# Second MoE of an attention and MoE chain: the first product as seven half-size products over halves of 256 tokens, Ln and Exp written into PSUM over h, output products one group later

## The chip, the cores and the metric

One Trainium2 chip, one of its cores. The time is device microseconds of one launch, inputs and outputs in HBM. Runs of the kernel before: median 1537.43 us of 3, from 1536.83 to 1538.73. One more execution was taken with the hardware profiler: 1537.71 us.

## The reference, cut to what matters

Attention first packs 576 keys into 32 per head and batch, and its output goes through two MoE blocks. The change is in the second:

```python
def _moe2_ref(x, w_in, w_out, a, b):          # x: 4608 x 512
    h = x @ w_in                              # 512 x 2048
    h2 = h * h
    h3 = h2 * h
    P = a[0] + a[1] * h + a[2] * h2 + a[3] * h3
    Q = 1.0 + np.abs(b[0]) * np.abs(h) + np.abs(b[1]) * h2
    g = P / (Q + 1e-06)
    return (g @ w_out).astype(np.float32)     # 2048 x 512
```

The first MoE has two products into 1536 features (gate and value) and one back to 512. All is f32. The kernel keeps a number as two f16 parts (high and low) and makes a product in three passes, high x high, high x low, low x high (`PASSES`).

## The kernel before, in words

The batches 0 to 7 go through attention and the first MoE. Its output x2 is written to HBM as two f16 parts, laid out in NB = 9 blocks of 512 tokens. All that up to the last batch is issued step by step in the order of one long string (`ORDER`): each word names a step of a few instructions. Every engine runs its own instructions in the order in which the program issues them, so this string sets the order of each engine and of the DMA queue. Beside the batches, the weights of the second MoE are decoded (they come as 64-bit words), split and stored to HBM: 16 tiles of w_in and 16 of w_out.

The last batch's gate and value tiles follow (L1127), with the loads of the 32 weight tiles, and then the second MoE, in plain loops. A chunk is 128 features of h for a block of 512 tokens; a block has 16. `h_mm` (L1414) makes a chunk in one PSUM bank: 12 matmuls of 512 columns. `stage_a` takes |h| and a linear term from it (ScalarE, L1426, L1427), then Q's first step on GpSimd (L1429), P's two steps on VectorE (L1432, L1433, which read h from PSUM) and Q's second step on VectorE (L1434). `stage_b`, one chunk later, has Ln and Exp (L1442, L1443, into SBUF) for 1/Q and three VectorE instructions (L1444 to L1446, all operands in SBUF). `stage_c`, two chunks later, splits g into two f16 parts (ScalarE L1451, GpSimd L1452).

The output product (`o_mm`, L1485) of a block runs one block behind: after chunk c of block j, TensorE makes chunk c of block j-1 for its four token tiles, 12 matmuls of 512 columns into four banks. At the block's end the four banks are evicted by ScalarE and VectorE (L1477, L1479) and stored. During block 0 the rest of the first MoE's output product (L1188) takes that place. The last block's output product comes at the end, one token tile after the other.

Of the kernel before, what the change touches and what calls it, by code (L numbers as in the profile page):

```python
# [1568 lines left out]
```

## Time and profile before

| | |
|---|---|
| profiled execution | 1537.71 us |
| its span, first to last instruction | 1535.9 us |
| TensorE busy | 1485.9 us (97%) |
| VectorE busy | 1304.3 us (85%) |
| ScalarE busy | 920.4 us (60%) |
| GpSimd busy | 576.7 us (38%) |
| granted TensorE clock, mean | 0.986 |

Busy times are shares of the whole span. The kernel has three stretches that differ: a start with many loads, the batches up to about 742 us, and the second MoE from there. A share says little about any one of them, so the rows below are taken by stretch. In the profile's rows PE is TensorE, DVE is VectorE, ACT is ScalarE and POOL is GpSimd. A clock of 1.00 is 2.4 GHz, 0.50 is 1.2 GHz.

### The profile page before, as it was taken

To read this page: it belongs to the slowest core of one execution; us is meant where nothing else is said; L and a number is where in the kernel's file an instruction comes from. 1 tells how busy PE (TensorE), PEld (TensorE's weight loads), DVE (VectorE), ACT (ScalarE), POOL (GpSimd) and SP (SyncE) were. 2 spreads that over 40 slices of the span, in tenths; PEclk is the share of its full clock that TensorE was granted. 3 is DMA by queue.
4 is the path that set the end of the run, shared out by engine and by line. 5 is a ranking of instruction groups with operands and counts; after the bars stand their busy time and mean duration, and the time that the engine had idled before them with its cause. 6 is when DMAs were issued, how large, how long until landed. Compare 5 with 4: busy or idle time off the path is not lost.

```text
span 1535.9 us, 28044 instructions
## 1 busy us (share of the span) xinstructions
PE 1485.9 (97%) x10644; PEld 887.6 (58%) x10644; DVE 1304.3 (85%) x2224; ACT 920.4 (60%) x1871; POOL 576.7 (38%) x663
## 2 busy tenths in 40 slices
...
GB/s 259 224 188 138 95 150 124 107 104 144 170 163 189 161 193 165 191 145 239 101 16 37 1 56 0 55 1 30 26 1 55 1 55 0 56 1 28 1 28 28
DMA packets 221911, 143.06 MB, mean 93 GB/s; under 512 B 162256, under 2 KB 199120, under 8 KB 220624
## 3 DMA queue, kind: packets, MB, share of 16 engines
...
## 4 chain that ended last, share of the span: by engine, by line
PE 80%; DVE 10%; DMA 3%; issue 2%; ACT 2%; POOL 1%; SPq 1%; POOLq 0%; DVEq 0%; ACTq 0%
PE h L1414 23%; PE o L1485 22%; PE o L1188 15%; PE gv L1127 13%; PE xo L891 1%; PE mm L417 1%; PE mm L415 1%; PE s L857 1%; DVE w L1444 1%; PE pk L811 1%; POOL y L1157 1%; DVE t L1145 1%; DVE v L749 1%; DVE t L1142 1%; DVE x16in L749 1%
## 5 line engine op out<-in xcount | busy, mean ns | idle before, releaser
L1485 PE MATMUL o<-w2o,g 128*128 128x512 f16 x1728 | 398.4, 381 | 6.5 <-DVE osb L1479 3.8
L1414 PE MATMUL h<-xi,w2i 128*128 128x512 f16 x1728 | 396.3, 379 | 0.0
L1127 PE MATMUL gv<-an,mt 128*128 128x256 f16 (+1 forms) x2304 | 305.2, 287 | 11.2 <-DVE t L1145 2.8
L1485 PEld LDWEIGHTS <-g 128*128 128x128 f16 x1728 | 169.4, 98 | 214.7 <-issue 8.8
L1188 PE MATMUL o<-y,wo 128*128 128x256 f16 (+1 forms) x2160 | 282.6, 286 | 2.8 <-POOL y L1157 1.9
L1414 PEld LDWEIGHTS <-w2i 128*128 128x128 f16 x1728 | 169.1, 98 | 200.9
L1127 PEld LDWEIGHTS <-mt 128*128 128x128 f16 x2304 | 222.0, 98 | 80.8 <-issue 25.7
L1188 PEld LDWEIGHTS <-wo 128*128 128x128 f16 x2304 | 224.5, 98 | 69.1 <-issue 7.2
L1157 POOL TENSOR_TENSOR y<-t,y 128x256 f16<-128x256 f32 (+1 forms) x180 | 151.9, 851 | 265.9 <-ACT y L1152 258.3
L1429 POOL TENSOR_SCALAR w<-ah,cf 128x512 f32<-128x512 f32 x144 | 110.6, 768 | 373.4 <-DVE t L1446 153.2
L1452 POOL TENSOR_TENSOR g<-t,g 128x512 f16<-128x512 f32 x144 | 174.5, 1211 | 99.5 <-issue 67.0
L1426 ACT ACTIVATE ah<-h 128x512 f32<-128x512 f32 x144 | 85.6, 594 | 207.4 <-PE h L1414 207.2
L1444 DVE SCALAR_TENSOR_TENSOR w<-w,r 128x512 f32<-128x512 f32 x144 | 180.0, 1250 | 3.9 <-ACT r L1443 3.9
L1434 DVE TENSOR_TENSOR w<-w,ah 128x512 f32<-128x512 f32 x144 | 134.9, 937 | 0.0
L1432 DVE TENSOR_TENSOR t<-t,h 128x512 f32<-128x512 f32 x144 | 98.4, 684 | 42.3 <-ACT t L1427 41.8
L1138 ACT ACTIVATE t<-gv 128x256 f32<-128x256 f32 (+1 forms) x192 | 76.6, 405 | 82.4 <-PE gv L1127 63.0
L1427 ACT ACTIVATE t<-h,cf 128x512 f32<-128x512 f32 x144 | 111.4, 774 | 22.5 <-POOL g L1452 22.3
L1142 DVE SCALAR_TENSOR_TENSOR t<-t,gv 128x256 f32<-128x256 f32 (+1 forms) x192 | 84.9, 448 | 40.1 <-ACT t L1138 39.3
L1433 DVE SCALAR_TENSOR_TENSOR t<-t,cf,h 128x512 f32<-128x512 f32 x144 | 107.7, 748 | 5.1
L1445 DVE SCALAR_TENSOR_TENSOR t<-t,cf,r 128x512 f32<-128x512 f32 x144 | 107.5, 747 | 0.0
L1446 DVE SCALAR_TENSOR_TENSOR t<-w,t 128x512 f32<-128x512 f32 x144 | 99.6, 692 | 4.9
L1442 ACT ACTIVATE r<-w,one 128x512 f32<-128x512 f32 x144 | 103.3, 717 | 0.0
...
## 6 DMA issues: line engine op xcount, KB each, us to landing
...
```

The lines of the kernel that those rows point to most:

```text
L1127: nc.tensor.matmul(out=ps, lhsT=mt[b, nm, c // 4, g][:, l, cs], rhs=an[b][:, 2 * r_ + g, cols], start=(n == 0), stop=(n == 5))
L1157: nc.gpsimd.tensor_tensor(out=y[:, 1], in0=t, in1=y[:, 0], op=ALU.subtract)
L1188: nc.tensor.matmul(out=ps, lhsT=wo1[c][:, l, d * 128:(d + 1) * 128], rhs=ys[b, h, c][:, r_, :], start=(c == 0 and n == 0), stop=(c == NF1 ...
L1414: nc.tensor.matmul(out=ps, lhsT=w[:, l, cs], rhs=x2in[j][:, r_, kc, :], start=(n == 0), stop=(n == 3 * KC - 1))
L1427: act(out=t, in_=ps, func=AF.Identity, scale=cf[:, 0:1], bias=cf[:, 7:8])
L1429: nc.gpsimd.tensor_scalar(out=w, in0=ah, scalar1=cf[:, 6:7], scalar2=cf[:, 5:6], op0=ALU.mult, op1=ALU.add)
L1433: stt(out=t, in0=t, scalar=cf[:, 1:2], in1=ps, op0=ALU.add, op1=ALU.mult)
L1434: nc.vector.tensor_tensor(out=w, in0=w, in1=ah, op=ALU.mult)
L1444: stt(out=w, in0=w, scalar=Q1, in1=r0, op0=ALU.add, op1=ALU.mult)
L1445: stt(out=t, in0=t, scalar=cf[:, 2:3], in1=r0, op0=ALU.add, op1=ALU.mult)
L1452: nc.gpsimd.tensor_tensor(out=g[:, 1], in0=t, in1=g[:, 0], op=ALU.subtract)
L1485: nc.tensor.matmul(out=ps, lhsT=gs[j, c][:, l, t * 128:(t + 1) * 128], rhs=w2t["o", 0, c][:, r_, :], start=(c == 0 and n == 0), stop=(c == ...
```

## The change

With x as halves of 256 tokens by halves of 256 inputs, and w_in as halves of 256 inputs by halves of 1024 features, the four quarters of h are sums of seven products instead of eight (Strassen's scheme in Winograd's form). A group (j, cp) is the unit now: two feature chunks in each half of the features, both token halves, so four banks A, B, C, D of 512 columns (two chunks of 256 tokens in each). A block has four groups; there are 36.

- Weights: seven combinations of w_in's quarters, 28 tiles instead of 16, made on GpSimd from the decoded tiles, split and stored as before; with w_out 44 tiles are stored and loaded.
- Tokens: x2 is kept as f32 in HBM (one ScalarE instruction evicts it, the VectorE instruction L1166 is gone). Per block four sums on VectorE (s3 to s6) and seven splits (h0 to h6 on ScalarE, l0 to l6 on GpSimd) make the seven operands.
- Products: 84 matmuls of 256 columns per group. Products 1, 6, 7 and 4 are added up in bank A, and ScalarE copies A to SBUF after 1, 6 and 7 (k1, k2, k3); 5 and 3 go into B, 2 into C. VectorE adds the copies: a1 writes bank D from B, a2 adds to C, a3 to B.
- Rational function: steps A (|h| and the linear term), w and W (Q on GpSimd, both steps), t and u (P), l and x (Ln and Exp, now into the bank of h), q, e, g (VectorE), h and i (the split). The number behind the letter is the tile, 0 to 3 for A, D, C, B.
- Output products: o0 to o3 in pieces of three matmuls, issued among the next group's products. f and F evict and store a token tile.
- Order: all of the kernel is issued from the string, which is new throughout. PSUM keeps 5 + 3 banks: three for A, B, C, five for D and the four output tiles.

```diff
-    x2_dram = [tc.dram_tile((128, 2, KC, BLK), F16, name=f"x2s{j}") for j in range(NB)]
+    x2_dram = [tc.dram_tile((128, KC, BLK), F32, name=f"x2s{j}") for j in range(NB)]
...
-        "wl2 wb2 wc2 wd2 0pl 0pf 0ph wl3 wb3 wc3 wl0 L0 0kf00 wb0 0kf01 0kg00 0kg01 wc0 L1 0kf02 wd3 0kf10 wd0 cc "
...
+        "wl9 wb9 0pl 0pf 0ph L1 0kf10 0kf12 0kg10 0kg12 wl7 wc9 wd9 0kf11 0kg11 0am1 cc L0 0kf00 wb7 0kg00 0kf01 "
...
+    def operands(j):
...
+        def hi(n, src):
+            act(out=flat(n, 0), in_=src(), func=AF.Copy)
...
+        def lo(n, src):
+            nc.gpsimd.tensor_tensor(out=flat(n, 1), in0=src(), in1=flat(n, 0), op=ALU.subtract)
+
+        def both(out, a, b, op):
+            nc.vector.tensor_tensor(out=out, in0=a, in1=b, op=op)
...
+        def product(x, p, e, first):
+            if first and e == 0:
+                bank(x)
+            fr, cs = divmod(2 * cp + e, 4)
+            n = 0
+            for kc in range(2):
+                w = w2t["t", p, 2 * fr + kc]
+                for l, r_ in PASSES:
+                    nc.tensor.matmul(
+                        out=st[x][:, W2 * e:W2 * e + W2], lhsT=w[:, l, 128 * cs:128 * cs + 128],
+                        rhs=xs[j][:, OPERAND[p], r_, kc], start=(first and e == 0 and n == 0), stop=(n == 5), skip_group_check=True,
+                    )
+                    n += 1
+
+        def keep(nm, x):
+            st[nm] = f32_tile("su")
+            act(out=st[nm], in_=st[x], func=AF.Copy)
+
+        def plus(out, a, b):
+            nc.vector.tensor_tensor(out=out, in0=a, in1=b, op=ALU.add)
+
+        for x, p, first in (("A", 1, True), ("A", 6, False), ("A", 7, False), ("A", 4, False), ("B", 5, True), ("C", 2, True), ("B", 3, False)):
...
-        nc.vector.tensor_tensor(out=w, in0=w, in1=ah, op=ALU.mult)
...
+        def s_q2():
+            nc.gpsimd.tensor_tensor(out=st["w", n], in0=st["w", n], in1=st["ah", n], op=ALU.mult)
...
-        r0 = st_p.tile([128, BLK], F32, tag="raw32", bufs=2, name="r0")
-        act(out=r0, in_=w, func=AF.Ln, bias=one[:, 0:1])
-        act(out=r0, in_=r0, func=AF.Exp, scale=-1.0)
-        stt(out=w, in0=w, scalar=Q1, in1=r0, op0=ALU.add, op1=ALU.mult)
-        stt(out=t, in0=t, scalar=cf[:, 2:3], in1=r0, op0=ALU.add, op1=ALU.mult)
-        stt(out=t, in0=w, scalar=-2.0, in1=t, op0=ALU.add, op1=ALU.mult)
...
+        def s_ln():
+            act(out=st[x], in_=st["w", n], func=AF.Ln, bias=one[:, 0:1])
+
+        def s_exp():
+            act(out=st[x], in_=st[x], func=AF.Exp, scale=-1.0)
+
+        def s_num():
+            stt(out=st["t", n], in0=st["t", n], scalar=cf[:, 2:3], in1=st[x], op0=ALU.add, op1=ALU.mult)
+
+        def s_err():
+            stt(out=st[x], in0=st["w", n], scalar=Q1, in1=st[x], op0=ALU.add, op1=ALU.mult)
+
+        def s_g():
+            stt(out=st["t", n], in0=st[x], scalar=-2.0, in1=st["t", n], op0=ALU.add, op1=ALU.mult)
```

In the middle of a later block the string repeats itself. The words of one group there (83: block 8, group 3; 82: the group before), product steps m, output pieces o:

```
g83m10 g82e1 g82A3 g82w2 g83m11 g82g1 g81o300 g82W2 g82t2 g83k1 g81o310 g82h1 g82u2 g83m60 g82i1 g82t3 g82l2 g83m61
...
g83m50 g83u0 g83W0 g83m51 g82o110 g82i3 g83l0 g83a1 g82o101 g83A1 g83m20 g83x0 g83m21 g83t1 g83w1 g82o111 g83q0 g83W1
```

ScalarE, the second MoE before: one chunk after the other, five instructions each (L1442 Ln, L1443 Exp, L1451 the high part, L1426 |h|, L1427 the linear term).

```order
L1442 ACTIVATE r_18130<-w,one 128x512 [waits DVE_49]
L1443 ACTIVATE r_18130<-r_18130 128x512 [waits Activation_49]
L1451 ACTIVATE g<-t_18036 128x512 [waits DVE_49]
L1426 ACTIVATE ah<-h 128x512 [waits PE_49]
L1427 ACTIVATE t_18165<-h,cf 128x512 [waits Pool_49]
```

ScalarE now, where one group ends and the next begins: Ln and Exp of tile 1 (hd is bank D), the linear pairs of tiles 2 and 3 (L1726, L1728), the first copy k1 of the next group's bank A (L1693), the high part of tile 1 and Ln of tile 2.

```order
L1745 ACTIVATE hd<-w,one 128x512 [waits DVE_49,Pool_49]
L1748 ACTIVATE hd<-hd 128x512 [waits Activation_49]
L1726 ACTIVATE ah<-h 128x512 [waits DVE_49]
L1728 ACTIVATE t<-h,cf 128x512
L1726 ACTIVATE ah<-h 128x512 [waits DVE_49]
L1728 ACTIVATE t<-h,cf 128x512
L1693 ACTIVATE su<-h 128x512 [waits PE_49]
L1761 ACTIVATE g<-t 128x512 [waits DVE_49]
L1745 ACTIVATE h<-w,one 128x512 [waits DVE_49,Pool_49]
```

The copy of bank A is a new kind of instruction for ScalarE, and it stands behind two linear pairs that wait for VectorE; on TensorE product 6 waits for it.

VectorE now, in the same stretch: a1 (L1696, into hd), step t of tile 1, q, e, g of tile 0, step u of tile 1, the two sums a2 and a3, and q, e, g of tile 1.

```order
L1696 TENSOR_TENSOR hd<-h,su 128x512
L1739 TENSOR_TENSOR t<-t,hd 128x512
L1751 SCALAR_TENSOR_TENSOR t<-t,cf,h 128x512
L1754 SCALAR_TENSOR_TENSOR h<-w,h 128x512
L1757 SCALAR_TENSOR_TENSOR t<-h,t 128x512
L1742 SCALAR_TENSOR_TENSOR t<-t,cf,hd 128x512
L1696 TENSOR_TENSOR h<-h,su 128x512 x2
L1751 SCALAR_TENSOR_TENSOR t<-t,cf,hd 128x512
L1754 SCALAR_TENSOR_TENSOR hd<-w,hd 128x512
L1757 SCALAR_TENSOR_TENSOR t<-hd,t 128x512
```

Every one of these has an operand in PSUM (h, hd); the sums are new, and the product of w and ah is no longer here.

GpSimd before, in the second MoE: two instructions by turns.

```order
L1429 TENSOR_SCALAR w<-ah,cf 128x512
L1452 TENSOR_TENSOR g<-t_18251,g 128x512
```

GpSimd now, in the first group of a block: three instructions per tile (L1731 and L1736 for Q, L1765 the low part of g), and between them low parts of the next block's operands (L1633, into xo).

```order
L1731 TENSOR_SCALAR w<-ah,cf 128x512
L1736 TENSOR_TENSOR w<-w,ah 128x512
L1633 TENSOR_TENSOR xo<-sx,xo 128x512
L1633 TENSOR_TENSOR xo<-xf,xo 128x512
L1765 TENSOR_TENSOR g<-t,g 128x512
L1633 TENSOR_TENSOR xo<-sx,xo 128x512
L1731 TENSOR_SCALAR w<-ah,cf 128x512
L1736 TENSOR_TENSOR w<-w,ah 128x512
L1765 TENSOR_TENSOR g<-t,g 128x512
L1633 TENSOR_TENSOR xo<-xf,xo 128x512 x2
```

The product L1736 came from VectorE, and the operand parts are gathered in one group of the four.

## Rows read from the trace of the kernel before

**Rows 1.** Table of stretches; stretch in us, its length, busy time of each engine (instructions).

```profile
core 0: us, PE busy (x) PEld busy (x) DVE busy (x) ACT busy (x) POOL busy (x), PEclk, DMA share, GB/s
0.00:100.00 100.00, 72.46 (x600) 46.74 (x600) 75.02 (x166) 48.26 (x114) 21.63 (x34) 0.85 0.77 228
100.00:704.00 604.00, 592.16 (x6014) 446.25 (x6015) 505.02 (x1116) 394.91 (x957) 252.33 (x314) 0.99 0.66 149
704.00:742.00 38.00, 38.00 (x314) 30.47 (x312) 23.40 (x54) 20.45 (x52) 19.44 (x27) 1.00 0.76 274
...
819.00:1481.00 662.00, 658.24 (x3047) 297.91 (x3045) 619.46 (x781) 397.82 (x651) 251.40 (x256) 1.00 0.07 23
1481.00:1536.00 55.00, 48.01 (x207) 20.30 (x205) 12.23 (x16) 7.68 (x13) 4.26 (x4) 0.94 0.12 39
```

**Rows 2.** Chain that ended last: start us, us, engine, tile, line, matmuls.

```profile
744.71 2.62 PE o L1188 x24
...
1085.08 2.59 PE o L1485 x12
...
1478.96 2.60 PE h L1414 x12
```

**Rows 3.** Order in time, one chunk: start us, us, engine, line, operation, out<-in, shapes.

```profile
1204.75 2.75 PE L1485 MATMUL o<-w2o,g 128*128 128x512 f16 x12
1204.95 0.60 ACT L1426 ACTIVATE ah<-h 128x512 f32<-128x512 f32 x1 [2.13 <-PE h L1414]
...
1205.44 0.77 ACT L1427 ACTIVATE t<-h,cf 128x512 f32<-128x512 f32 x1
1206.10 0.72 ACT L1442 ACTIVATE r<-w,one 128x512 f32<-128x512 f32 x1
1206.25 0.69 DVE L1432 TENSOR_TENSOR t<-t,h 128x512 f32<-128x512 f32 x1 [0.16 <-ACT t L1427]
1206.27 0.77 POOL L1429 TENSOR_SCALAR w<-ah,cf 128x512 f32<-128x512 f32 x1 [2.12 <-ACT t L1427]
1206.85 0.63 ACT L1443 ACTIVATE r<-r 128x512 f32<-128x512 f32 x1
1206.97 0.75 DVE L1433 SCALAR_TENSOR_TENSOR t<-t,cf,h 128x512 f32<-128x512 f32 x1
...
1207.39 0.61 ACT L1451 ACTIVATE g<-t 128x512 f16<-128x512 f32 x1
1207.63 0.68 DVE L1434 TENSOR_TENSOR w<-w,ah 128x512 f32<-128x512 f32 x1
1208.14 1.19 POOL L1452 TENSOR_TENSOR g<-t,g 128x512 f16<-128x512 f32 x1 [1.11 <-issue]
1208.23 1.65 DVE L1444 SCALAR_TENSOR_TENSOR w<-w,r 128x512 f32<-128x512 f32 x1
...
1209.81 0.74 DVE L1445 SCALAR_TENSOR_TENSOR t<-t,cf,r 128x512 f32<-128x512 f32 x1
...
1210.58 0.69 DVE L1446 SCALAR_TENSOR_TENSOR t<-w,t 128x512 f32<-128x512 f32 x1
```

**Rows 4.** One line's instructions: engine, count, duration ns min/median/max, first and last start.

```profile
L1432 DVE TENSOR_TENSOR t<-t,h x144: 677/682/690, 746.0 to 1482.9; 128x512 f32<-128x512 f32 x144
...
L1444 DVE SCALAR_TENSOR_TENSOR w<-w,r x144: 676/1645/1650, 753.2 to 1493.0; 128x512 f32<-128x512 f32 x144
```

**Rows 5.** The same view for L1166 and L375.

```profile
L1166 DVE SCALAR_TENSOR_TENSOR x2e<-o,x2e x64: 406/438/492, 127.5 to 818.8; 128x256 f16<-128x256 f32 x32, 128x320 f16<-128x320 f32 x32
...
L375 ACT ACTIVATE xo<-xo x35: 567/582/598, 166.5 to 702.6; 128x512 f32<-128x512 f32 x28, 64x512 f32<-64x512 f32 x7
```

**Rows 6.** Groups by line: count | busy us, mean ns | idle before, us.

```profile
L1321 POOL TENSOR_TENSOR raw<-raw,raw 128x512 f16<-128x512 f32 x32 | 40.4, 1264 | 50.2 <-ACT raw L1317 34.1 <-DVE x2e L1166 6.3 <-DVE sum L331 4.3
```

**Rows 7.** Order in time: the end of a block, and the last block's output product.

```profile
903.52 1.46 PE L1485 MATMUL o<-w2o,g 128*128 128x512 f16 x6 [0.54 <-DVE osb L1479]
...
1498.02 33.78 PE L1485 MATMUL o<-w2o,g 128*128 128x512 f16 x145 [0.25 <-POOL g L1452]
```

More of the change, by code (lines that the diff above doesn't have):

```diff
@@ L1327, in w2_pieces, with add, minus_of @@
         steps = {}
-        for n in range(len(w2_items)):
-            for nm, f in (
-                ("uL", lambda n: w2.load(n, nc.sync)), ("ub", w2.step), ("uc", w2.step), ("ud", w2.step),
-                ("uA", w2_scale), ("uH", w2_hi), ("uP", w2_lo), ("uS", w2_store),
+        def add(tag, key, src, dst):
+            for nm, f in zip("HPS", w2_split(key, src, dst)):
+                steps[f"u{nm}{tag}"] = f
+        def minus_of(out, a, b):
+            return lambda: nc.gpsimd.tensor_tensor(out=out(), in0=a(), in1=b(), op=ALU.subtract)
@@ L1384, in attention_pack_glu_rational_kernel @@
-    assert not w2_left and len(w2.dec) == len(w2_items)
-    last1 = itertools.chain(out1_slots(B - 1, 0), out1_slots(B - 1, 1))
-    an_p.release()
-    mt_p.release()
-    xi_p = sb("xi", "right")
-    g_p = sb("g", "left")
-    t2_p = sb("t2", "left")
-    ps_h = tc.alloc_tile_pool(name="ps_h", bufs=3, space=PSUM, side="right", reuse_waits="tile")
-    x2in = {}
-    def load_x2(j):
-        if j < NB:
-            t = xi_p.tile([128, 2, KC, BLK], F16, tag="xi", bufs=2, name="xi")
-            nc.sync.dma_start(out=t, in_=x2_dram[j])
-            x2in[j] = t
@@ L1403, in attention_pack_glu_rational_kernel @@
-    nc.scalar.preload_act_table_set("natural_log_exp_and_others")
-    gs = {}
-    pend = {}
-    def h_mm(j, c):
-        ps = ps_h.tile([128, BLK], F32, tag="h", name="h")
-        n = 0
-        for kc in range(KC):
-            w = w2t["i", c // 4, kc]
-            cs = slice((c % 4) * 128, (c % 4) * 128 + 128)
-            for l, r_ in PASSES:
-                nc.tensor.matmul(
-                    out=ps, lhsT=w[:, l, cs], rhs=x2in[j][:, r_, kc, :], start=(n == 0), stop=(n == 3 * KC - 1)
-                )
-                n += 1
-        return ps
@@ L1455, in late, with w2_load @@
-    def late(i):
-        if 0 <= i - 1 < NB * NF2:
-            stage_b(*divmod(i - 1, NF2))
-        if 0 <= i - 2 < NB * NF2:
-            stage_c(*divmod(i - 2, NF2))
-    one = const.tile([128, 1], F32, name="one")
-    nc.vector.memset(one, Q1)
+    NG = NF2 // 4
+    LAST = B - 1
+    one = const.tile([128, 1], F32, name="one")
+    Q1 = 1.0 + 1e-6
+    nc.vector.memset(one, Q1)
+    p2 = {}
+    late = []
+    xs, gs, po = {}, {}, {}
+    def w2_load(key):
+        t = w2t[key] = w2_p[0].tile([128, 2, 512], F16, name="w2{}_{}_{}".format(*key))
+        nc.sync.dma_start(out=t, in_=w2_dram[key])
@@ new lines, in attention_pack_glu_rational_kernel, with group, bank, mid @@
+    OPERAND = (None, 0, 1, 6, 2, 3, 4, 5)
+    TILES = ((1, 0), (1, 1), (0, 0), (0, 1))
+    def group(j, cp):
+        st = {}
+        steps = {}
+        W2 = BLK // 2
+        def bank(x):
+            if x == "D":
+                st[x] = ps_m.tile([128, BLK], F32, tag="m", name="hd")
+            else:
+                st[x] = ps_h[0].tile([128, BLK], F32, tag="h", bufs=3, name="h")
+        def product(x, p, e, first):
[9 more added lines that the diff above has]
+                        rhs=xs[j][:, OPERAND[p], r_, kc], start=(first and e == 0 and n == 0), stop=(n == 5), skip_group_check=True,
+                    )
+                    n += 1
[5 more added lines that the diff above has]
+        for x, p, first in (("A", 1, True), ("A", 6, False), ("A", 7, False), ("A", 4, False), ("B", 5, True), ("C", 2, True), ("B", 3, False)):
+            for e in range(2):
+                steps[f"m{p}{e}"] = lambda x=x, p=p, e=e, first=first: product(x, p, e, first)
+        steps["k1"] = lambda: keep("s1", "A")
+        steps["k2"] = lambda: keep("u2", "A")
+        steps["k3"] = lambda: keep("u3", "A")
+        def mid():
+            bank("D")
+            plus(st["D"], st["B"], st["u3"])
+        steps["a1"] = mid
+        steps["a2"] = lambda: plus(st["C"], st["C"], st["s1"])
+        steps["a3"] = lambda: plus(st["B"], st["B"], st["u2"])
+        for n, x in enumerate("ADCB"):
+            rational(steps, st, n, x, j, cp)
+        for n in range(4):
+            e, f = TILES[n]
+            for t in range(2):
+                for i in range(2):
+                    steps[f"o{n}{t}{i}"] = lambda n=n, t=2 * e + t, u=t, i=i, c=2 * cp + 8 * f + i: o_mm(j, t, gs[j, cp, n], u, i, c)
+        return {f"g{j}{cp}{nm}": f for nm, f in steps.items()}
@@ L1471, in token_rows @@
         return [(0, 128, rows[r])]
[L1473 to L1483 removed]
+    done = {}
@@ L1484, in o_mm @@
+    def o_mm(j, t, g, u, i, c):
+        k = j, t
+        if k not in po:
+            po[k] = ps_m.tile([128, DM], F32, tag="m", name="o")
+            done[k] = 0
         for n, (l, r_) in enumerate(PASSES):
             nc.tensor.matmul(
-                out=ps,
-                lhsT=gs[j, c][:, l, t * 128:(t + 1) * 128],
-                rhs=w2t["o", 0, c][:, r_, :],
-                start=(c == 0 and n == 0),
-                stop=(c == NF2 - 1 and n == 2),
-            )
-    ps_o = [None]
@@ L1524, in attention_pack_glu_rational_kernel @@
-    for i in range(2):
-        late(NB * NF2 + i)
-    for t in range(4):
-        ps = ps_o[0].tile([128, DM], F32, tag="o", name="o")
-        for c in range(NF2):
-            o_mm(ps, NB - 1, t, c)
-        finish(NB - 1, t, ps, "act" if t % 2 else "dve")
-    for pool in (t2_p, g_p, x2_p, tmp_p, y_p, wo1_p, st_p, const, xi_p, w2_p, yl_p[0], ps_o[0], ps_h):
+                out=po[k], lhsT=g[:, l, 256 * i + 128 * u:256 * i + 128 * u + 128], rhs=w2t["o", 0, c][:, r_, :],
+                start=(done[k] == 0), stop=(done[k] == 3 * NF2 - 1),
+            )
@@ new lines, in o_mm, with o_evict, o_store @@
+            done[k] += 1
+    osb = {}
+    def o_evict(j, t):
+        if t % 2:
+            o = st_p.tile([128, 512], I64, tag="raw64", bufs=STAGES, name="osb").bitcast(F32)[:, 0:DM]
+        else:
+            o = st_p.tile([128, DM], F32, tag="raw32", bufs=2, name="osb")
+        osb[j, t] = o
+        sc = 1.0 / (S_G * S_WO2)
+        if t % 2:
+            act(out=o, in_=po[j, t], func=AF.Copy, scale=sc)
+        else:
+            nc.vector.tensor_scalar_mul(o, po[j, t], sc)
+    def o_store(j, t):
+        for p0, n, dst in token_rows(4 * j + t):
+            nc.sync.dma_start(out=dst, in_=osb[j, t][p0:p0 + n])
@@ new lines, in attention_pack_glu_rational_kernel @@
+    for x in w2_keys:
+        p2["wL{}{:x}{:x}".format(*x)] = lambda x=x: w2_load(x)
+    for j in range(NB):
+        p2 |= operands(j)
+        for cp in range(NG):
+            p2 |= group(j, cp)
+        for t in range(4):
+            p2[f"f{j}{t}"] = lambda j=j, t=t: o_evict(j, t)
+            p2[f"F{j}{t}"] = lambda j=j, t=t: o_store(j, t)
+    steps |= p2
+    w2_p, xf_p, xo_p = [], [], [None, None]
+    seg = [x.split() for x in ORDER.split("|")]
+    for nm in seg[0]:
+        steps[nm]()
```

283 lines of the change are left out of this document (144 added, 139 removed), and 547 rows, old and new, of the table ORDER.

## The prediction

> **What bounds the kernel now.** I read the table of stretches first, then the chain of waits, then the order in time of one chunk, then the spread of single lines.
>
> In the table [rows 1] the reader is to see that TensorE is never free for long. In the second MoE (819 to 1481 us) it is busy 658.24 of 662.00 us at a granted clock of 1.00, the 2.4 GHz level. From 100 to 704 us it lacks 11.84 us. Only the first 100 us (27.5 us idle, clock 0.85) and the last 55 (7.0 us idle, clock 0.94) are worse. VectorE follows closely: 619.46 us of the same 662.
>
> The chain of waits [rows 2] says the same with prices. In the second MoE it runs through TensorE alone, tile after tile of 12 matmuls in 2.59 us, so a matmul of 512 columns costs 0.2158 us. The first MoE's matmuls of 256 columns, each with its own weight load, take 2.62 us for 24, so 0.1092 us. That is 1.2% over half, and it is what half-width products pay.
>
> The order in time of one chunk [rows 3] shows why TensorE could not simply be made faster before: a chunk's two tiles take TensorE 5.18 us, and VectorE's six instructions add up to 5.20. One of the six is swollen: L1444 takes 1.65 us, and began 0.09 us after GpSimd's L1452 (1.19 us). Its spread is 676 to 1650 ns, while L1432, which takes h from PSUM, stays within 677 to 690 ns though GpSimd's L1429 runs beside it [rows 3, 4].
>
> **The change, part by part.**
>
> *First product.* 1728 matmuls of 512 columns go: 1728 x 0.2158 = 372.9 us. 9 blocks x 4 groups x 84 = 3024 of 256 columns come: 3024 x 0.1092 = 330.2 us. **-42.7 us** of TensorE, which is on the path throughout. The 1728 of the output product stay. TensorE's floor for a group (four tiles) becomes 84 x 0.1092 + 48 x 0.2158 = 19.53 us, against 20.72 before. That only counts if three other engines stay under 19.53.
>
> *VectorE.* Gone: L1434 (it moves to GpSimd) and all 64 of L1166, 438 ns each, 28 us [rows 5]. Added: three sums per group, four per block. By start-to-start times [rows 3], a tile costs 0.72 + 0.66 + 0.66 + 0.72 + 0.60 = 3.36 us (0.72 where the next instruction needs the result). Four tiles and three sums at 0.60 make 15.2 us, and the block's four sums and two evictions add 0.9 per group: 16.1 of 19.53. This takes every instruction at its unswollen length, because all but the four sums now have one operand in PSUM, like L1432. A VectorE instruction that writes PSUM has no row here; the nearest are 0.60 (L1434) and 0.77 us (L1445 to L1446) start to start, and I take 0.60 to 0.72.
>
> The Trainium skill (SBUF — State Buffer, "SBUF: two separate sides") says that a VectorE instruction with two SBUF inputs and a GpSimd instruction that reads SBUF lock each other out for a whole instruction. The 1.65 us fits. If the lock took every VectorE instruction, the eight two-input instructions that GpSimd now has per group, at up to 0.96 us each (1.65 less 0.69), would put VectorE at 23.8 us and nothing would be gained; by the 677 to 690 ns of L1432 it does not.
>
> *ScalarE.* Per tile 0.49 + 0.66 + 0.75 + 0.54 = 2.44 us by the starts in [rows 3], and 0.54 for the split, as after Exp: 2.98. Four tiles, three copies at 0.49 and about 1.1 for the block's operands: 14.5 of 19.53. Ln and Exp now write PSUM. L375, PSUM to PSUM, takes 582 ns [rows 5], less than the 0.63 us of L1443 [rows 3], so I charge nothing; bounds -0.05 to +0.15 us each.
>
> *GpSimd.* Per tile 0.77 + 1.15 + 1.15 us: L1429, the moved product, and L1452 (1.19 less the 0.04 that it waits). That is 12.3 per group. The moved product, f32 from two f32 inputs, has no row. Below lies L1429 with one input (0.77), above L1321's mean under contention (1.26) [rows 3, 6]; scaled by bytes it could reach 1.55. I take 1.15, the nearest in kind.
>
> The Trainium skill (GPSIMD Engine Reference, "Elementwise — side-by-side cycle accounting") puts such an instruction at about twice VectorE's time; an estimate by it is 2 x 0.68 = 1.37 us, which would add some 4 us to the total. No run here shows it yet.
>
> Seven operand splits per block (1.19 us each) come on top, six of them in one group: 12.3 + 7.1 = 19.4 of 19.53. There GpSimd is full, and a Ln waits behind it, then the third copy behind the Ln, then product 4 on TensorE. I charge **1.1 us x 8 blocks = +8.8** (0 if the queue drains in time, 3 each at 1.55 us).
>
> *The wait added in every group.* Bank A takes products 1, 6, 7, 4 one onto another, with a ScalarE copy between them, so product 6 queues on TensorE behind the first copy, and everything after it behind product 6. That copy stands on ScalarE behind both linear pairs of the group before. From the end of product 5 to product 6 of the next group the chain is, by the starts and ends in [rows 3]: 0.20 until VectorE sees the bank, 0.73 sum, 0.49 and 0.81 the linear pair, 0.60, 0.66, 0.72, 0.60 on VectorE, 0.79 the next, 0.75 Ln, 0.54 Exp, two linear pairs 2.30, 0.60 copy, 0.04 back to TensorE: 9.83 us. TensorE has nine output pieces (3 x 0.2158) and six product pieces (6 x 0.1092) to do meanwhile: 9.76 us. So 0.1 us shows, and I charge 0.15: **36 x 0.15 = +5.4 us**. The cover is all but used up: whatever lengthens the chain shows in full.
>
> *Boundaries and tail.* Before, TensorE waits at the end of each block for the eviction (0.54 us at 903.52 [rows 7]) and lacks 3.8 us in all from 819 to 1481. After, evictions come one pair at a time while other pieces run: **-3.8**. At the end, the last block's output product waits for the last chunk: 145 matmuls from 1498.02 take 33.78 us, 0.233 each, since the clock had fallen after the idle stretch. From the end of the last h tile (1481.6 [rows 2]) 204 matmuls of 0.2158 would end at 1525.6; they end at 1531.8. With the output products one group behind, I see 0.6 of these 6.2 us left: **-5.6**.
>
> *Start of the second MoE.* 28 + 16 weight tiles are loaded instead of 32, with the first block: 12.6 MB, at the 274 GB/s of 704 to 742 us [rows 1] 46 us. They lie beside some 60 us of TensorE work of the last batch, so hidden. But the first group has little besides it, and the new tiles wait for the old weights and y to be done: **+3** (0 to 8).
>
> *First MoE.* TensorE's 6928 matmuls before 742 us [rows 1] are the same, in another order. VectorE loses 28 us, ScalarE gets 12 more splits, GpSimd 12 splits and 16 differences (28 x 1.26 = 35 us, of which it has room), the SP queue 12 more stores. With 11.8 us idle from 100 to 704 there is little to win, and a new order can lose: **0**, bounds -8 to +10.
>
> **Sum.** -42.7 - 3.8 - 5.6 + 5.4 + 8.8 + 3 + 0 = -34.9. The profiled execution took 1537.7 us (span 1535.9 and 1.8 around it), 0.3 above the median of the runs shown. So 1537.7 - 34.9 = 1502.8: I say 1503.
>
> **Rivals.**
>
> *The cover is gone.* Each PSUM write on VectorE or ScalarE costs 0.05 us more, or the moved product takes 1.5 us, and the chain shows 0.6 us more in each of 34 groups: +20, 1523 us. For it: 9.83 against 9.76 us leaves no slack. Against: L375 and L1432 show PSUM no slower.
>
> *Slower: ScalarE and VectorE pace each other.* The same chain at 11.5 us instead of 9.83 makes TensorE wait 1.75 us in front of product 6 in each group; 34 x 1.6 = 54 more, 1557 us. It decides from about 10.9 us, where the wait has eaten the 35 us (36 x 0.97). For it: some 17 links in a row across two in-order engines, so 0.06 us more on each suffices. Against: each link has a row of its own with no slack hidden in it.
>
> *Better: the first MoE gains too.* VectorE, busy 505 of 604 us there, is relieved by 28, the first keys are loaded behind one weight tile instead of three, and half of the idle time from 100 to 704 us and the waits at the start of the second MoE vanish: 6 + 3 and some 3 at the first keys, -12, 1491 us. For it: VectorE ends many of the waits before 704 us. Against: an order made for other reasons.
>
> *It doesn't do what it says.* If weight loads showed between half-width products, at 0.1205 us each instead of 0.1092, the 42.7 us would shrink to 8.5 and the other terms (+7.8) would eat them: 1537 us. Against it stand the 0.1092 us themselves, measured with one load each.
>
> **How the numbers follow.** The forecast (1495 to 1512) 0.60, cover gone (1512 to 1530) 0.15, slower 0.10, better 0.12, no effect 0.03. A measurement of this kernel can tell 0.2%, 3 us, from no change. Faster: 0.60 + 0.15 + 0.12 = 0.87; same 0.03; slower 0.10. The range runs from 1488 to 1524: it leaves out the slower case, no effect and the ends of the others.
>
> **What would show it.** In the profile after: the first product's matmuls 0.109 us apart; VectorE's rational instructions all under 0.8 us, the one that was 1.65 too; the moved product on GpSimd near 1.15 us; groups 19.6 to 19.8 us apart, one per block about 20.8; TensorE's waits in the second MoE named after ScalarE's copies, 10 to 20 us in all. The prediction is wrong if groups without operand splits are over 20.2 us apart, if TensorE lacks over 20 us more before the second MoE than it did, or if VectorE's sums wait in line for GpSimd.

## The result, and the profile after

| | before | changed |
|---|---|---|
| median of four runs, us | 1537.85 (1536.83 to 1538.73) | 1500.89 (1499.25 to 1503.34) |
| ratio, 95% interval | | 0.9761 (0.9744 to 0.9778) |
| span of the profiled execution, us | 1535.9 | 1499.0 |

The forecast was 1503. First the table of stretches, to be read against [rows 1] (columns as there; the second MoE ends at 1481 and the program at 1499).

```profile
0.00:100.00 100.00, 77.73 (x640) 52.22 (x641) 76.57 (x174) 50.30 (x121) 19.54 (x33) 0.90 0.81 231
100.00:704.00 604.00, 583.22 (x5939) 440.51 (x5937) 501.58 (x1053) 397.51 (x961) 286.03 (x346) 1.00 0.66 154
704.00:742.00 38.00, 37.66 (x350) 31.85 (x348) 15.55 (x36) 15.09 (x37) 13.55 (x17) 1.00 0.61 209
742.00:819.00 77.00, 76.85 (x596) 57.98 (x594) 49.14 (x80) 51.04 (x94) 44.82 (x45) 1.00 0.29 100
819.00:1481.00 662.00, 652.35 (x4363) 426.25 (x4361) 544.88 (x806) 478.85 (x820) 488.19 (x452) 1.00 0.07 25
1481.00:1499.00 18.00, 13.85 (x65) 6.05 (x62) 10.09 (x16) 7.13 (x12) 6.67 (x6) 0.94 0.16 58
```

TensorE stays the busiest engine in every stretch but is idle more than before in two of them: 20.8 us from 100 to 704 (11.8 before) and 9.65 from 819 to 1481 (3.76 before). In the second MoE GpSimd went from 251 to 488 us, VectorE from 619 down to 545.

The answer to [rows 3] for TensorE, order in time: the group behind the one with the operands' low parts, then part of an ordinary group. From block 2 on a group's products come on TensorE in the order 1, 6, 7, 4, 5, 2, 3.

```profile
1185.94 1.47 PE L1685 MATMUL h<-xo,w2t 128*128 128x256 f16 x12 [1.28 <-ACT su L1693]
1187.25 1.46 PE L1789 MATMUL o<-w2o,g 128*128 128x512 f16 x6
...
1189.85 1.46 PE L1789 MATMUL o<-w2o,g 128*128 128x512 f16 x6
1191.72 1.47 PE L1685 MATMUL h<-xo,w2t 128*128 128x256 f16 x12 [0.41 <-ACT su L1693]
...
1206.11 1.47 PE L1685 MATMUL h<-xo,w2t 128*128 128x256 f16 x12
...
1214.57 1.47 PE L1685 MATMUL h<-xo,w2t 128*128 128x256 f16 x12
1215.88 1.46 PE L1789 MATMUL o<-w2o,g 128*128 128x512 f16 x6
```

A product's twelve matmuls take 1.31 us from start to start of the rows (1185.94 to 1187.25), 0.109 each. Product 6 starts at 1206.11 and product 5 ends at 1215.88, 9.77 us. Product 6 of the next group comes 19.60 us after 1206.11, so 9.83 after that end. These are the 9.76 and 9.83 of the prediction. A block takes 80.34 us (from the first of these waits to the next block's, five times), so 80.34 - 4 x 19.60 = 1.94 more than four ordinary groups. It stands in front of products 6 (1185.94) and 4 (1191.72) of one group, behind the copies k1 and k3. The view of waits has nothing else for TensorE from 819 us on:

```profile
PE h L1685 <- ACT su L1693: 9.6, 12, 1.3
```

VectorE, ScalarE and GpSimd in the chain, where a group's bank D is worked on, and (above it) in the group with the low parts (L1633):

```profile
1177.35 2.28 POOL L1633 TENSOR_TENSOR xo<-xf,xo 128x512 f16<-128x512 f32 x2
...
1180.47 1.27 POOL L1736 TENSOR_TENSOR w<-w,ah 128x512 f32<-128x512 f32 x1
...
1181.77 0.69 ACT L1745 ACTIVATE hd<-w,one 128x512 f32<-128x512 f32 x1 [1.09 <-POOL w L1736]
...
1205.44 0.62 ACT L1693 ACTIVATE su<-h 128x512 f32<-128x512 f32 x1
...
1218.12 0.69 DVE L1739 TENSOR_TENSOR t<-t,hd 128x512 f32<-128x512 f32 x1 [1.33 <-ACT t L1728]
1218.37 1.27 POOL L1736 TENSOR_TENSOR w<-w,ah 128x512 f32<-128x512 f32 x1
...
1220.71 0.74 DVE L1742 SCALAR_TENSOR_TENSOR t<-t,cf,hd 128x512 f32<-128x512 f32 x1
...
1221.54 0.69 ACT L1745 ACTIVATE hd<-w,one 128x512 f32<-128x512 f32 x1
```

In the ordinary group Ln of tile 1 starts at 1221.54, 0.09 after u (L1742), although its operand from L1736 was there at 1219.64: it writes the bank that u reads. In the group with the low parts it waits for L1736, behind two L1633.

The spreads that answer to [rows 4] and [rows 6]: the three rational instructions on VectorE and the moved product.

```profile
L1751 DVE SCALAR_TENSOR_TENSOR t<-t,cf,h x105: 730/746/749, 796.6 to 1487.9; 128x512 f32<-128x512 f32 x105
L1754 DVE SCALAR_TENSOR_TENSOR h<-w,h x105: 679/689/691, 797.2 to 1488.6; 128x512 f32<-128x512 f32 x105
L1757 DVE SCALAR_TENSOR_TENSOR t<-h,t x105: 674/691/693, 798.0 to 1489.3; 128x512 f32<-128x512 f32 x105
L1736 POOL TENSOR_TENSOR w<-w,ah x140: 1267/1276/1587, 793.0 to 1483.5; 128x512 f32<-128x512 f32 x140
```

Not one of the 315 is over 0.75 us; L1444 before was 1.65. The tail, against the 145 matmuls of [rows 7]:

```profile
1479.80 15.06 PE L1789 MATMUL o<-w2o,g 128*128 128x512 f16 x69
```

### The profile page after: what moved, and what is told of

It is laid out like the page before. It is cut to its first block, busy times and chain, and to the rows that moved or that the text cites. A ratio compares the mean times of both kernels' runs of the same rounds, so it can differ in the third digit from the quotient of the medians.

```text
span 1499.0 us, 31046 instructions
## 1 busy us (share of the span) xinstructions
PE 1441.7 (96%) x11940; PEld 1014.9 (68%) x11940; DVE 1197.8 (80%) x2160; ACT 999.9 (67%) x2042; POOL 858.8 (57%) x898
## 4 chain that ended last, share of the span: by engine, by line
PE 67%; DVE 13%; POOL 9%; ACT 6%; issue 3%; DMA 2%; SPq 0%; ACTq 0%; DVEq 0%; POOLq 0%
PE o L1789 17%; PE h L1685 15%; PE o L1393 14%; PE gv L1340 13%; POOL xo L1633 2%; POOL w L1736 2%; POOL g L1765 2%; POOL w L1731 1%; PE xo L891 1%; DVE raw L135 1%; PE mm L415 1%; DVE t L1358 1%; PE mm L417 1%; PE pk L811 1%; DVE t L1355 1%
## 5 line engine op out<-in xcount | busy, mean ns | idle before, releaser
L1685 PE MATMUL h<-xo,w2t 128*128 128x256 f16 x3024 | 368.6, 272 | 9.8 <-ACT su L1693 9.6
L1685 PEld LDWEIGHTS <-w2t 128*128 128x128 f16 x3024 | 295.4, 98 | 97.9 <-issue 17.6
L1765 POOL TENSOR_TENSOR g<-t,g 128x512 f16<-128x512 f32 x140 | 167.8, 1199 | 115.4 <-ACT g L1761 115.4
L1736 POOL TENSOR_TENSOR w<-w,ah 128x512 f32<-128x512 f32 x140 | 178.7, 1278 | 10.8
L1731 POOL TENSOR_SCALAR w<-ah,cf 128x512 f32<-128x512 f32 x140 | 109.0, 779 | 58.1 <-ACT ah L1726 58.1
L1761 ACT ACTIVATE g<-t 128x512 f16<-128x512 f32 x140 | 88.5, 634 | 62.0 <-DVE t L1757 62.0
L1355 DVE SCALAR_TENSOR_TENSOR t<-t,gv 128x256 f32<-128x256 f32 (+1 forms) x192 | 84.5, 446 | 52.4 <-ACT t L1351 51.4
L1362 ACT ACTIVATE y<-t 128x256 f16<-128x256 f32 (+1 forms) x192 | 81.8, 437 | 62.6 <-DVE t L1358 61.4
L1745 ACT ACTIVATE h<-w,one 128x512 f32<-128x512 f32 x105 | 72.9, 695 | 69.7 <-POOL w L1736 51.6
L1751 DVE SCALAR_TENSOR_TENSOR t<-t,cf,h 128x512 f32<-128x512 f32 x105 | 78.1, 743 | 48.1 <-ACT h L1748 46.9
L1358 DVE SCALAR_TENSOR_TENSOR t<-t,gv 128x256 f32<-128x256 f32 (+1 forms) x192 | 84.5, 448 | 39.1 <-PE gv L1340 33.1
L1728 ACT ACTIVATE t<-h,cf 128x512 f32<-128x512 f32 x105 | 82.3, 783 | 0.8 <-POOL g L1765 0.8
L1742 DVE SCALAR_TENSOR_TENSOR t<-t,cf,h 128x512 f32<-128x512 f32 x105 | 78.4, 747 | 3.4
L1726 ACT ACTIVATE ah<-h 128x512 f32<-128x512 f32 x108 | 64.5, 597 | 22.1 <-PE h L1685 13.9
```

What stands on the lines that cost most here:

```text
L1355: stt(out=t, in0=t, scalar=1.0, in1=ps_g, op0=ALU.add, op1=ALU.mult)
L1358: stt(out=t, in0=t, scalar=S_Y / (2.0 * (S_AN * S_M) ** 2), in1=ps_v, op0=ALU.mult, op1=ALU.mult)
L1685: nc.tensor.matmul(out=st[x][:, W2 * e:W2 * e + W2], lhsT=w[:, l, 128 * cs:128 * cs + 128], rhs=xs[j][:, OPERAND[p], r_, kc], start=(first ...
L1728: act(out=st["t", n], in_=st[x], func=AF.Identity, scale=cf[:, 0:1], bias=cf[:, 7:8])
L1731: nc.gpsimd.tensor_scalar(out=st["w", n], in0=st["ah", n], scalar1=cf[:, 6:7], scalar2=cf[:, 5:6], op0=ALU.mult, op1=ALU.add)
L1736: nc.gpsimd.tensor_tensor(out=st["w", n], in0=st["w", n], in1=st["ah", n], op=ALU.mult)
```

## The experiments

**Half width by itself.** The kernel before, each matmul of h in two halves:

```diff
-out=ps, lhsT=w[:, l, cs], rhs=x2in[j][:, r_, kc, :]
+out=ps[:, hs], lhsT=w[:, l, cs], rhs=x2in[j][:, r_, kc, hs]     # for each of two halves hs of 256
```

> The kernel before with the first product's matmuls in halves of 256 columns, 24 per chunk instead of 12, nothing else. The price of half width by itself. Theory, 0.1092 us each: 1728 x (2 x 0.1092 - 0.2158) = 4.5 us, all on TensorE's path: 1541 to 1543. Rival, weight loads show between half-width products, 0.1205 each as in the case that would have eaten the gain: 43.5 us more, 1581.

1544.0 us, ratio to before 1.0032 (1.0020 to 1.0045): 4.9 us more, from 3.1 to 6.9; 1.2% of the 372.9 us would be 4.5. TensorE's idle time from 819 to 1481 is 3.56 us as against 3.76. The price is that of the term, and no weight load shows.

**Product 3 left out.**

```diff
             n = 0
+            if p == 3:
+                return
```

> The changed kernel with the twelve matmuls of product 3 left out in every group (the output lacks it): 432 matmuls of 256 columns, 1.31 us a group. Theory, the chain sets the period: from product 6 to the end of product 5 TensorE takes 9.77 us, and from there the chain through VectorE and ScalarE to the copy k1 takes 9.83, whatever TensorE does meanwhile; product 3 lies in that cover, so the period stays at 19.6 and TensorE waits 1.2 to 1.3 us for k1 in each group: 1497 to 1502. Rival, TensorE's own work sets it: 36 times 1.31 is 47 us, 1454. Half of each: some links give way, 1475.

1502.26 us, ratio 0.9765 (0.9738 to 0.9792), the same as with the product. TensorE's rows (1201.55 and 1221.14 are the same product of two groups):

```profile
1201.55 1.47 PE L1687 MATMUL h<-xo,w2t 128*128 128x256 f16 x12
1202.86 1.46 PE L1791 MATMUL o<-w2o,g 128*128 128x512 f16 x6
1205.53 1.47 PE L1687 MATMUL h<-xo,w2t 128*128 128x256 f16 x12 [1.21 <-ACT su L1695]
...
1221.14 1.04 PE L1687 MATMUL h<-xo,w2t 128*128 128x256 f16 x8
```

19.59 us, with 1.21 of waiting where the twelve matmuls were. Nearly all of the 47 us of saved work turned into waits for k1 (43.6 us listed, in 32 waits). TensorE is 96% busy in the changed kernel, and yet the chain sets the period.

**Ln and Exp into SBUF again.**

```diff
-            act(out=st[x], in_=st["w", n], func=AF.Ln, bias=one[:, 0:1])
+            st["r", n] = f32_tile("r")
+            act(out=st["r", n], in_=st["w", n], func=AF.Ln, bias=one[:, 0:1])
```

and r instead of the bank in Exp, q and e, w instead of the bank in e and g.

> The changed kernel with Ln and Exp written into an SBUF tile again, so that q, e and g (L1751, L1754, L1757) have both operands in SBUF, while GpSimd has three instructions per tile. Theory, such VectorE instructions and GpSimd's two-input instructions hold each other up, as the 1.65 us of L1444 before: one in three swollen by 0.96 us makes VectorE 3.8 us longer per group, 19.9 of 19.6, and the chain through q, e, g of tile 0 shows: 1535 to 1590; all three swollen would be 1780. In the trace the three are far above 0.75 us. Rival, PSUM as the place of 1/Q made no difference, and only the moved product relieved VectorE: 1499 to 1504, the three at 0.69 to 0.75 us.

1612.25 us, ratio 1.0479 (1.0439 to 1.0520), above the expected range. The three rational instructions and GpSimd's two for Q, in the order of the program's lines:

```profile
L1754 DVE SCALAR_TENSOR_TENSOR t<-t,cf,r x140: 735/1228/1710, 803.9 to 1602.0; 128x512 f32<-128x512 f32 x140
L1757 DVE SCALAR_TENSOR_TENSOR w<-w,r x140: 676/684/1753, 804.6 to 1602.6; 128x512 f32<-128x512 f32 x140
L1760 DVE SCALAR_TENSOR_TENSOR t<-w,t x140: 676/1061/1646, 805.3 to 1603.3; 128x512 f32<-128x512 f32 x140
L1733 POOL TENSOR_SCALAR w<-ah,cf x140: 757/1052/1732, 798.3 to 1595.1; 128x512 f32<-128x512 f32 x140
L1738 POOL TENSOR_TENSOR w<-w,ah x140: 1263/1582/1727, 799.1 to 1596.3; 128x512 f32<-128x512 f32 x140
```

Same operations, same sizes: with both operands in SBUF VectorE's instructions take up to 1.75 us, and GpSimd's medians go from 0.77 to 1.05 and from 1.28 to 1.58. Both engines pay. The place of 1/Q is worth 111 us, three times the gain of the whole change. The new ring of two r tiles is not what costs: ScalarE waits for it three times, 5.2 us in all. Part of the 111 us is slower matmuls behind the waits, since the granted clock from 819 to 1590 us is 0.96, against 1.00 in the changed kernel; that part was not taken apart.

**The product w times |h| on VectorE again.**

```diff
-            nc.gpsimd.tensor_tensor(out=st["w", n], in0=st["w", n], in1=st["ah", n], op=ALU.mult)
+            nc.vector.tensor_tensor(out=st["w", n], in0=st["w", n], in1=st["ah", n], op=ALU.mult)
```

> The changed kernel with the product w times |h| (L1736) back on VectorE. It has both operands in SBUF and stands on VectorE between q and e of tile 0 and the like, so in the chain from product 5 to k1. Theory, the chain is 0.66 us longer by it, and by up to 1.0 more where GpSimd holds it up, and shows in full: groups of 20.3 to 21.2 us, 25 to 58 us more, less the 8 to 10 us of the waits behind GpSimd's low parts: 1516 to 1550. Rival, VectorE has room for it (16.2 + 4 x 0.68 = 18.9 of 19.6) and GpSimd gets free: 1491 to 1500.

1563.76 us, ratio 1.0161 (1.0136 to 1.0185): the side was right, the size too small by 14 us.

```profile
L1736 DVE TENSOR_TENSOR w<-w,ah x140: 673/684/1635, 793.4 to 1546.0; 128x512 f32<-128x512 f32 x140
```

Most of the 140 are not swollen at all, and VectorE has room for them. It is their place in the chain that costs: in one group (product 6 at 1268.50 and, 21.18 us later, at 1289.68) one of them, 1.07 us long, stands ahead of the sum a1 and one between q and e of tile 0. Over the second MoE TensorE's waits for k1, k2 and k3 are 43.5 us, and 15.6 more came up in front of products that wait for g of tile 0 (L1757), a wait the expectation did not have.

**The low parts spread, first try.** In blocks 2 to 7 four of the six low parts move to the second and third group, and with them the load of the next operands and their first two sums:

```diff
-... g43g2 x6l0 g43o010 ... g50x0 x6l5 g50m20 ... F42 x6l2 x6h6 ... g50x1 x6l1 g50A2 ... x6l6 x7L ... g51k3 g50o010 x7s3 ... g50i2 x7s5
+... g51A0 x6l0 ... g51x0 x6l5 ... g52A0 x6l2 ... g52x0 x6l1 x7L ... g52g3 x7s3 ... g53l0 x7s5
```

> The changed kernel with four of the six low parts of the next block's operands (GpSimd, L1633) taken out of a block's first group and put into its second and third, in blocks 2 to 7; all work of ScalarE and VectorE on the operands stays in the first group. Theory, GpSimd's queue: in the changed kernel TensorE waits for the copy k1 and for k2 or k3 only in the group after these low parts (six times 1.28 us or 0.83, and 0.41), and those waits hang on a Ln behind the product L1736 behind the low parts. They then go: minus 8 to 9.5 us, 1491 to 1493. Rival, ScalarE's five high parts and VectorE's two swollen sums (1.58 and 1.04 us) fill the group: the waits stay, 1499 to 1502.

1497.55 us, ratio 0.9731 (0.9706 to 0.9756), a third of what was expected. The old waits were gone and a new one stood in the next block's first group. VectorE's rows of the two sums, and TensorE's of the wait:

```profile
1153.36 0.68 DVE L1640 TENSOR_TENSOR sx<-xf 128x512 f32<-128x512 f32 x1
...
1155.33 1.50 DVE L1640 TENSOR_TENSOR xf<-xf 128x512 f32<-128x512 f32 x1
...
1166.37 1.47 PE L1689 MATMUL h<-xo,w2t 128*128 128x256 f16 x12 [1.41 <-ACT su L1697]
```

The edit had put the two sums into the chain.

**The low parts spread, the two sums in VectorE's idle time** ahead of q of tile 3:

```diff
-... g52g3 x7s3 ... g53l0 x7s5
+... g52o010 x7s3 ... g52i2 x7s5 g52q3
```

> The low parts spread over three groups as before, but the two sums of the operands after next (L1636, s3 and s5) now stand in VectorE's idle stretch of some 2 us ahead of q of tile 3, not in the chain (there they cost 0.68 and 1.50 us and TensorE waited 1.40 us for k1 once per block). Theory, GpSimd's queue was what held the group of the operands, and the wait that stayed when the low parts were spread was those two sums: the waits go, 1489 to 1493. Rival, ScalarE's five high parts and VectorE's swollen sums of the first group: a wait of about 1.3 us per block stays, 1496 to 1500.

1490.57 us, ratio 0.9693 (0.9668 to 0.9718). TensorE has no listed wait left from block 2 on; groups are 19.60 us apart, one per block 19.75. ScalarE's high parts and VectorE's other two sums had stayed in the first group, and the two sums that moved had stood behind k3, so behind both waits; what had held TensorE was GpSimd's queue.

**k1 earlier**, and with the low parts spread:

```diff
-... g52m10 g51e1 g51A3 g51w2 g52m11 g51g1 ... g51t2 g52k1 ...
+... g52m10 g51e1 g52m11 g52k1 g51A3 g51w2 g51g1 ... g51t2 ...
```

> The changed kernel with the first copy k1 of a group ahead of the linear pair of tile 3 of the group before on ScalarE (product 1 is issued where it was on TensorE). Theory, the chain from product 5 to product 6 sets the period of 19.60 us: it gets 1 us shorter, so the ordinary groups fall to TensorE's 19.53 (35 times 0.07, 2.5 us) and the six waits of 1.28 us shrink by 0.6 or so: 1494 to 1498. Rival, the linear pair that is now 1 us later holds up the Ln of tile 3 and the bank for product 5 of the group after: TensorE waits there, 1503 to 1520.

> Both edits, the low parts spread and k1 ahead of the linear pair. If both theories hold, TensorE has no wait left in blocks 2 to 7 and groups are 19.53 to 19.55 us apart: 1488 to 1490. If only GpSimd's queue matters, as the low parts spread alone; if the linear pair's delay shows, slower than that by 10 us or more.

1519.29 us (ratio 0.9876, 0.9846 to 0.9905) and 1514.37 (0.9840, 0.9819 to 0.9862): slower by 18 and 14 us than the changed kernel. In five groups (the last of block 0 and all of block 1) this order puts the copy behind product 6, so bank A holds another sum there. Groups are 20.12 us apart. ScalarE's rows in one, and product 7's first matmul:

```profile
1214.30 0.78 ACT L1732 ACTIVATE t<-h,cf 128x512 f32<-128x512 f32 x1
...
1216.21 0.58 ACT L1752 ACTIVATE h<-h 128x512 f32<-128x512 f32 x1
1216.70 0.59 ACT L1697 ACTIVATE su<-h 128x512 f32<-128x512 f32 x1
1217.35 0.27 PE L1689 MATMUL h<-xo,w2t 128*128 128x256 f16 x1 [0.16 <-ACT su L1697]
```

The first copy is in time; the pair that it passed now stands, with the high part, Ln and Exp, in front of the second copy, and product 7 waits for that. The rival had the right culprit and the wrong place.

**u of tile 1 earlier**, in 27 groups:

```diff
-... g51t1 g51w1 ... g51g0 g51m31 g51u1 g51h0 ... g51l1 ... g51x1 ...
+... g51t1 g51u1 g51w1 ... g51g0 g51l1 g51m31 g51x1 g51h0 ...
```

> The changed kernel with step u of tile 1 (L1742) right behind step t on VectorE, ahead of q, e, g of tile 0, and Ln and Exp of tile 1 ahead of the high part of tile 0 on ScalarE, in 27 of the 36 groups. In the changed kernel Ln of tile 1, which writes the bank that u reads, starts 0.09 us after u ends although its other operand has been there for some 1.9 us. Theory, the chain from product 5 to the copy k1 sets the period, and this link is in it: the ordinary groups lose their 0.07 us and come to TensorE's 19.53 (27 times 0.07, 2 us), the six waits of 1.28 us behind GpSimd's low parts stay: 1496 to 1499. Rival, g of tile 0 is now 0.7 us later, and bank A with it: product 1 waits, 1503 to 1515.

1508.07 us, ratio 0.9803 (0.9776 to 0.9829), slower by 7. Ordinary groups came to 19.53 us, as the theory had it, but a block to 81.63: around the group with the low parts TensorE waits three times, for k1, k2 and k3, and not for bank A at product 1, where the rival had it.

```profile
1191.72 1.47 PE L1688 MATMUL h<-xo,w2t 128*128 128x256 f16 x12 [1.31 <-ACT su L1696]
1195.74 1.47 PE L1688 MATMUL h<-xo,w2t 128*128 128x256 f16 x12 [1.25 <-ACT su L1696]
1198.96 1.25 PE L1688 MATMUL h<-xo,w2t 128*128 128x256 f16 x10 [0.45 <-ACT su L1696]
```

There Ln waits for GpSimd anyway (2.42 us, to 1187.04), and now the high part of tile 0 stands behind it, at 1188.25; GpSimd, next in line with the low part of that tile, is idle for 1.95 us. That this is the link was not tried by itself; with the low parts spread, leaving those groups as they were removes the waits that are left (below).

> The low parts spread with the two sums in the idle stretch, and u of tile 1 early. Theory: neither the chain nor GpSimd holds TensorE from block 2 on, groups are 19.53 us apart and a block 78.1 (80.34 in the changed kernel, so 2.2 less for each of six or seven blocks): 1486 to 1490. Rival, something else has been close behind, the banks or VectorE's order: 1491 to 1500.

1491.12 us, ratio 0.9687 (0.9661 to 0.9713): 19.53 us in ordinary groups, but 0.8 us more around the group with the high parts, so no better than the low parts spread alone.

**Low parts spread, u early in the 21 other groups.**

> The low parts spread with the two sums in the idle stretch, and u of tile 1 early in the 21 groups that hold no high parts of operands (in the group with them the early u made waits of 0.8 us a block, since Ln of tile 1 waits for GpSimd there and stood ahead of the high part of tile 0). Theory, the chain from product 5 to k1 is what lies above TensorE's 19.53 us: ordinary groups 19.53, the one with the high parts 19.75 or less, so some 21 times 0.07, 1.5 us, less than with the low parts spread alone: 1487 to 1490. Rival, the two edits disturb each other in the groups next to it as well: 1491 to 1494.

1489.67 us, ratio 0.9674 (0.9648 to 0.9701): faster than the changed kernel, whose interval lies above. From the low parts spread alone (0.9668 to 0.9718) the times do not tell it apart; the trace does. A row of the table of stretches, and the same product in three groups running, with the high parts (1154.70 to 1168.04) between the first and the last:

```profile
819.00:1440.00 621.00, 621.00 (x4174) 408.15 (x4173) 519.42 (x772) 461.40 (x786) 466.57 (x434) 1.00 0.08 26
```

```profile
1143.71 1.47 PE L1688 MATMUL h<-xo,w2t 128*128 128x256 f16 x12
...
1163.24 1.47 PE L1688 MATMUL h<-xo,w2t 128*128 128x256 f16 x12
...
1182.77 1.47 PE L1688 MATMUL h<-xo,w2t 128*128 128x256 f16 x12
```

19.53 us each, the floor of 84 x 0.1092 + 48 x 0.2158. Here TensorE is the bound, in the group with the high parts too.

**The sums of the weights left out.**

```diff
-            steps[f"uT{x}1"] = minus_of(up(b12), dec(b12), dec(b11))      # and three more
+            for k in "1234":
+                steps[f"uT{x}{k}"] = lambda: None
-                ... (5, up(b12), half(b12, 0)), (6, up(b22), half(b12, 1)),
+                ... (5, dec(b12), half(b12, 0)), (6, dec(b22), half(b12, 1)),
```

> The changed kernel without the 16 differences of w_in's quarters on GpSimd (L1534, 22 us in all); the splits take plain quarters in their place, so the products are of other weights. TensorE was idle for 20.8 us from 100 to 700 us, 11.8 in the kernel before. Theory, GpSimd's new work there holds up VectorE's instructions on SBUF (L135, L749, L911, L794 are longer than before by some 15 us in all) and the first MoE's products with them: idle time falls to 12 to 16 us, 1492 to 1497. Rival, the order of the steps makes those waits: idle stays at 19 to 22 us, 1498 to 1502.

1492.72 us, ratio 0.9699 (0.9679 to 0.9719): 8.2 us less than the changed kernel. The row for 100 to 704 us:

```profile
100.00:704.00 604.00, 589.60 (x6025) 447.52 (x6025) 495.93 (x1064) 401.00 (x970) 265.77 (x332) 1.00 0.66 157
```

TensorE's idle time there is 14.4 us, 20.8 in the changed kernel; from 100 to 700 us it is 14.1, and 18.4 to 20.9 in the other kernels of this study that share the changed kernel's first MoE. VectorE is 5.7 us less busy, though it gets further. So 16 GpSimd instructions made half or more of what the first MoE lost. Whether they did it by lengthening VectorE's instructions or by holding up GpSimd's own queue is not separated, and what made the rest, the new order among other things, was not tried by itself.

## Why the prediction was right

The time and the mechanism hold in the second MoE: half-width products cost what a matmul of 256 columns had cost in the first MoE, and the chain is longer than TensorE's work by a hair, so that from block 2 on it sets the period. Step by step:

| step | predicted, us | measured, us |
|---|---|---|
| first product | -42.7 | 0.1092 each, as taken |
| block boundaries | -3.8 | -3.8: no wait for an eviction is left |
| tail | -5.6 | -5.3: 2.8 less idle, 145 matmuls at 0.216 and not 0.233 |
| k1 in every group | +5.4 | +2.0: 28 x (19.60 - 19.53), blocks 2 to 8 |
| GpSimd full once per block | +8.8 | +11.2: 1.94 in five blocks, 1.5 in one |
| start of the second MoE | +3 | +0.5 |
| first MoE | 0 | +3.7: 5.3 less idle in the first 100 us, 8.9 more to 704 |

The right column adds up to -34.4; the spans differ by 36.9. The 2.5 us left are in no row. A possible place, not shown, is the granted clock: from 20 to 80 us it is 0.70 to 0.77 before and 0.73, 0.76 and 1.00 after. That the forecast came within 2 us is partly luck: the misses of k1 (-3.4), GpSimd (+2.4), the start (-2.5), the first MoE (+3.7) and this rest (-2.5) nearly cancel.

*The cover.* 9.83 against 9.76 us was right to a hundredth, and not by errors that cancel: in the ordinary group from 1215.88 to 1225.72 no link is more than 0.05 us off its forecast (the largest are Exp, 0.49 for 0.54, and u to Ln, 0.83 for 0.79). Leaving product 3 out showed that this chain sets the period: without cover it shows in full. The term was sized 0.15 per group and is 0.07, the difference itself; the rounding up had no row. It also had it in all 36 groups: in blocks 0 and 1 the string has another order, and there 662 matmuls of 256 and 378 of 512 columns fill the time from 789.9 to 943.9 us without a wait.

*GpSimd.* The moved product takes 1.276 us, not 1.15: the step took the f16-writing L1452 as the nearest in kind. The Trainium skill (GPSIMD Engine Reference, "Elementwise — side-by-side cycle accounting") gave an estimate of 1.37 by its factor of two; the trace lies between the two, nearer to the page. The prediction put the whole wait in front of product 4, behind the third copy. There the trace lists 0.41 us; the larger part, 1.28, is in front of product 6, behind the first copy, since the Ln that GpSimd holds up first is that of tile 1, a link of the chain (1181.77). It also had the wait in 8 blocks of 1.1 us: it is in 6 of up to 1.94 (the long group of a block takes 21.5 us, forecast 20.8), since the string spreads the low parts in the first two, so two errors partly cancel.

*VectorE.* This was the step that decided. L1432's 677 to 690 ns next to a GpSimd instruction said that one operand in PSUM is enough to keep clear of the swelling, and all 420 new rows agree. What the Trainium skill says (SBUF — State Buffer, "SBUF: two separate sides") of two SBUF inputs against a GpSimd instruction that reads SBUF, the SBUF version of the same kernel shows: up to 1.75 us instead of 0.69.

*First MoE: the step that failed.* It counted 28 us of L1166 off VectorE and 35 us onto GpSimd "of which it has room", and put the sum at 0. From 100 to 704 us VectorE is busy 501.6 us, 505.0 before, although 24 us of L1166 had stood there: added up line by line, some 19 of them came back as longer instructions. Room on GpSimd was not free: without the 16 differences TensorE has 6.4 of the 8.9 us back that it had lost. Two lines of VectorE from 100 to 700 us (count | busy us, mean ns | idle before), each before, after, and after without the differences:

```profile
L749 DVE SCALAR_TENSOR_TENSOR v<-raw,v 128x256 f16<-128x256 f32 x56 | 31.3, 574 | 0.2 <-ACT v L740 0.2
...
L911 DVE SCALAR_TENSOR_TENSOR n<-d,rms,n 128x128 f16<-128x128 f32 (+1 forms) x66 | 23.2, 393 | 8.3 <-ACT n L905 8.3
```

```profile
L749 DVE SCALAR_TENSOR_TENSOR v<-raw,v 128x256 f16<-128x256 f32 x56 | 33.0, 600 | 2.6 <-ACT v L740 2.5
...
L911 DVE SCALAR_TENSOR_TENSOR n<-d,rms,n 128x128 f16<-128x128 f32 (+1 forms) x66 | 28.9, 483 | 3.7 <-ACT n L905 3.5
```

```profile
L911 DVE SCALAR_TENSOR_TENSOR n<-d,rms,n 128x128 f16<-128x128 f32 (+1 forms) x70 | 30.6, 482 | 5.9 <-ACT n L905 5.6
L749 DVE SCALAR_TENSOR_TENSOR v<-raw,v 128x256 f16<-128x256 f32 x56 | 29.1, 531 | 2.3 <-ACT v L740 2.3
```

L749 got shorter without the differences, L911, which had grown most, did not: its 90 ns have another cause, which stays open. The waits that grew are TensorE's for VectorE's gate and value steps: listed 3.8 us before, 13.8 after and 10.2 without the differences. The rival with a gain in the first MoE fell by this, though its gain at the first keys came.
